# Gated attention and MLP mixer on one core: the last unit's end by halves of queries, two token tiles evicted by ScalarE and POOL, and one weight block copied instead of loaded

## The chip, the cores and the metric

The kernel runs on one core of one Trainium2 chip. Its engines are TensorE (PE, matmuls into the eight banks of PSUM), VectorE (DVE), ScalarE (ACT), GpSimd (POOL) and SyncE (SP), each with its own queue of instructions that it takes in order; SP and ACT also issue DMA transfers from their queues. An instruction can stand in its queue waiting for semaphores, and then everything behind it in that queue stands too. The metric is the device time of one execution in microseconds, shown as the median of several runs.

## What is computed

The input is x, 2048 tokens of 448 features. Sixteen attention heads of 28 features share one key and one value head (multi-query attention); beside it stands a mixer with token shifts and an MLP; a sigmoid gate of each token blends both. All of it is float32.

```python
g = _sigmoid((x * gate_w).sum(-1, keepdims=True))
a = _A_ref(x, A_wq, A_wk, A_wv, A_wo)     # attention, then @ wo
b = _B_ref(x, B_w1, B_w2, B_w3, B_w4)     # shifts and MLP
return g * a + (1 - g) * b
# in _A_ref
scores = jnp.einsum("bhqd,bkd->bhqk", q, k) * (Dh ** -0.5)
p = _softmax(scores, axis=-1)
o = jnp.einsum("bhqk,bkd->bhqd", p, v)
# in _B_ref
h2 = _gelu(_layernorm(x1, axis=-1) @ w3) @ w4
return x1 + h2
```

## The kernel before

The first part of the program (to about 165 us) makes queries, keys, values and the token mixing. The second part is the MLP, in four blocks of 512 tokens (`b`) and 14 blocks of 128 hidden features (`f`). Float32 products are done as three products of a rounded high part and a low part (`w4h` and `w4l`, `gh` and `gl`), so each weight block is loaded raw (`raw3`, `raw4` in a tile `w34raw`) and split: ACT writes the high part, DVE the rest (`split_w4`). For the last two hidden blocks of the last token block a plain float32 copy of their w4 rows, `w4f`, is used later (`w4_half`); before the change it comes by a DMA of its own at `b == 2`, `f == 2`.

The third part is the attention, in 16 units `u` (four blocks of 512 queries times four groups of four heads). A unit goes over 16 key tiles `kt` of 128 keys. For each key tile PE makes the scores of the four heads in four PSUM banks (`scores`). ACT takes the exponential of three of them straight from PSUM (`p`); DVE copies the fourth to SBUF (`pd`) and ACT takes its exponential there, two key tiles at once (`late_exps`). PE then multiplies with the values, four heads side by side in 32 columns each, by halves of 256 queries (`value`, `values`); the value tile has a column of ones, so that the sums of the softmax come out as a row. DVE adds each pair of key tiles to an accumulator `o` (`add_value`). Some units later `o` is divided by its sums (`norm`) and multiplied with a quarter of wo (`wo_job` for a token tile of 128, `wo_half` for half its 448 columns); the product, times the gate, is added to the output tile `ot_n`, and after the fourth group the tile is stored.

That eviction has two forms. `by_one` is one DVE instruction: bank times gate plus `before`. `by_two` is an ACT instruction that writes bank times gate to a tile `y`, and a POOL addition of `y` to `ot`. Before the change `by_two` serves one tile, token tile 0 of the last unit, and there is one tile `y`.

The end of the program (from `toks = ...`) treats the last two key tiles (14 and 15) of the last unit, u = 15. Its accumulator is normalised in a shorter way than the others: PE transposes `o` by token tiles so that the sums lie along partitions (`tail_sums`), DVE takes reciprocals and spreads them to 32 columns (`rx`), PE transposes them back (`tail_spread`), and DVE multiplies `o` with them (`on`). `tail_sums(0)` and `tail_spread(0)` serve the first half of the queries (token tiles 0 and 1), those with 1 the second (2 and 3). Between them stand the last two halves of unit 14's product (`wo_half(u - 1, 3)` and `wo_half(u - 1, 7)`), and then the four `wo_job` of unit 15, whose tiles `ot_12` to `ot_15` are stored by four DMAs: `ot_12` and `ot_14` from ACT's queue, `ot_13` and `ot_15` from SP's. At the very end DVE writes a flag `redo` (all sums were in range), each engine loads it and branches, and SP waits for the DMA semaphores.

The order of instructions on each engine is that of the program text: the schedule is manual. PSUM banks are handed out by a list `banks`: `take()` takes the first, and a bank is appended when its last reader has been issued.

Of the kernel before, what the change touches and what calls it, by code (L numbers as in the profile page):

```python
# [9 lines left out]
F32 = mybir.dt.float32  # L10
F32R = mybir.dt.float32r
AF = mybir.ActivationFunctionType
ALU = mybir.AluOpType
# [3 lines left out]
P = 128  # L17
S = 2048
D = 448
# [5 lines left out]
NT = S // P  # L25
NF = F // P
NE = D // 32
NG = H // 4
SCALE = DH ** -0.5
# [8 lines left out]
def f32(ap):  # L38
    return ap.bitcast(F32)
# [3 lines left out]
def gated_mix_kernel(  # L43
# [206 lines left out]
    with tc.tile_pool(name="s1b", bufs=1) as s1b, \  # L250
# [347 lines left out]
        def split_w4(i):  # L598
            nc.scalar.copy(w4h[i], raw4[i])
            nc.vector.tensor_tensor(w4l[i], raw4[i], f32(w4h[i]), ALU.subtract)  # L600

# [44 lines left out]
    with tc.tile_pool(name="s2", bufs=1, reuse_waits="tile") as s2, \  # L646
# [47 lines left out]
        for b in range(NB):  # L694
            acc = [ps2.tile([P, 512], F32, tag="acc", bufs=4, name=f"acc_{b}_{t}") for t in range(4)]
            gs = {}
            for f in range(NF):
# [22 lines left out]
                if b == NB - 1 and f == 4:  # L720
                    weigh_x1(0, 4 * b)
                if b == 2 and f == 2:
                    nc.sync.dma_start(w4f, w4[(NF - 2) * P:NF * P, :].rearrange("(c p) n -> p c n", p=P))
                if b == 1 and f in (0, 2, 4, 6):
# [44 lines left out]
    with tc.tile_pool(name="s3", bufs=1, reuse_waits="tile") as s3, \  # L769
# [53 lines left out]

        ot_of = {}

        def by_two(n, ps, before, cols):
            nc.scalar.activation(y, ps[:, cols], AF.Copy, scale=gg[:, n:n + 1])
            nc.gpsimd.tensor_tensor(ot_of[n], y, before, ALU.add)

# [25 lines left out]

        def wo_half(u, i, then=None):
            t, h = divmod(i, 2)
            wo_job(u, t, slice(224 * h, 224 * h + 224), then=then)

# [77 lines left out]
        pd_free = [s3.tile([P, 2, 512], F32, name=f"pd_{i}") for i in range(PD)]  # L937
        y = s3.tile([P, D], F32, name="y")
        ones1 = s3.tile([P, 1], F32, name="ones1")
# [5 lines left out]
        def turn_of(free):  # L945
            t = free.pop(0)
            free.append(t)
            return t

        def last_exps(kt, bs, parts):  # L950
            ps = p_of[NU - 1, kt] = {j: turn_of(p_free) for j in READ}
            for q in parts:
                for j in READ:
                    nc.scalar.activation(ps[j][:, q], bs[j][:, q], AF.Exp, scale=SCALE)

# [17 lines left out]

        def value(u, kt, q, pv):
            for j in range(4):
                nc.tensor.matmul(pv[32 * j:32 * j + 32, q], vext[:, kt, :], p_of[u, kt][j][:, q],  # L976
                                 start=(kt % 2 == 0), stop=(kt % 2 == 1), tile_position=(0, 32 * j))

# [4 lines left out]
        def values(u, v):  # L983
            if v == 0:
                o_of[u] = s3.tile([P, 512], F32, tag="o", bufs=2, name=f"o_{u}")
            for q in HALVES:
                pv = take()
                for kt in (2 * v, 2 * v + 1):
                    value(u, kt, q, pv)
# [55 lines left out]
        def tail_sums(i):  # L1045
            ps = take()
            for k in range(2):
                nc.tensor.transpose(ps[:, P * k:P * k + P], o[:, toks[2 * i + k]], ident)
            sums = ps[:, 0:2 * P].rearrange("p (k j d) -> p k j d", k=2, j=4)[:, :, :, 0]
            nc.vector.reciprocal(rr[:, i], sums)  # L1050
            nc.vector.tensor_copy(rx[:, i], rr[:, i].unsqueeze(3).broadcast_to([P, 2, 4, 32]))
            return sums, ps
# [14 lines left out]
        toks = [slice(t * P, (t + 1) * P) for t in range(4)]  # L1067
        bs = [scores(u, kt) for kt in (NT - 2, NT - 1)]
        last_exps(NT - 2, bs[0], [slice(0, 512)])
        banks.extend(bs[0][j] for j in READ)  # L1070
        last_exps(NT - 1, bs[1], HALVES)
        values(u, v - 1)
        pvs = [take(), take()]
        for i, q in enumerate(HALVES):
            value(u, NT - 2, q, pvs[i])
        value(u, NT - 1, HALVES[0], pvs[0])
        add_value(u, HALVES[0], pvs[0])
        wo_half(u - 1, 3)
# [83 lines left out]
```

## Time and profile before

| what | value |
|---|---|
| median of 3 runs | 913.67 us (913.38 to 913.93) |
| the profiled execution's own time | 914.09 us |
| its span, first to last instruction | 912.3 us |
| busy: DVE, ACT, POOL | 542.5, 633.4, 106.7 us |
| DMA traffic | 52.27 MB, mean 57 GB/s |
| mean granted TensorE clock | 0.999 |

The span leaves out 1.79 us of the execution's own time (914.09 - 912.3), which lie before the first and after the last instruction. The timeline of an engine gives start, duration, line, operation, the tiles written and read, and in brackets the idle time before it and what ended it; rows with "x8" merge that many instructions that follow one another. The table of windows gives each engine's busy time in a stretch of the span, the granted clock, the share in which the DMA engines were busy, and the bytes they moved per second.

### The profile page before, as it was taken

What the parts mean: (1) busy time and instruction counts of PE and PEld (TensorE: products, weight loads), DVE (VectorE), ACT (ScalarE), POOL (GpSimd) and SP (SyncE); (2) the same over time, 40 slices, a digit from 0 to 9 for tenths busy, and PEclk for the clock granted to TensorE, in tenths of its full rate; (3) what the DMA queues carried; (4) which work ended last, traced back from release to release, by engine and by line L of the source; (5) the groups of instructions that cost most, each with busy time, mean ns of one, the idle gap of its engine ahead of it and who ended that gap; (6) DMA issues with size and microseconds to landing.
All of it is one profiled execution on the core that took longest, in us unless ns stands there. A gap on an engine that the chain in (4) does not pass through costs nothing.

```text
span 912.3 us, 24128 instructions
## 1 busy us (share of the span) xinstructions
PE 905.2 (99%) x10093; PEld 642.2 (70%) x10093; DVE 542.5 (59%) x1086; ACT 633.4 (69%) x1134; POOL 106.7 (12%) x138
## 2 busy tenths in 40 slices
PE   9999999999999999999999999999999999999997
PEld 7788888888888888875565565556556555655663
DVE  4665264631435736456666766666667766666774
ACT  5442255322232232159999999999999999999994
POOL 3143200212000430002200000000000000000000
PEclk9999999999999999999999999999999999999999
DMA  9832543220222042120000001000011000110001
GB/s 299 271 101 44 158 149 122 40 67 21 41 80 60 21 103 62 37 65 14 26 26 3 26 14 57 24 26 26 6 43 46 26 3 26 29 53 3 15 14 43
DMA packets 42080, 52.27 MB, mean 57 GB/s; under 512 B 9328, under 2 KB 27824, under 8 KB 41968
## 3 DMA queue, kind: packets, MB, share of 16 engines
q1 hardware_dynamic: 38800, 45.00, 17.5%
q10 hardware_dynamic: 3168, 5.70, 1.8%
q8 instruction: 80, 1.31, 0.6%
q14 instruction: 32, 0.26, 0.1%
HBM read 37.50 MB, written 11.93 MB: 54 GB/s over the span
## 4 chain that ended last, share of the span: by engine, by line
PE 99%; ACT 0%; DVE 0%; issue 0%; DVEq 0%; ACTq 0%
PE bank L976 24%; PE bank L933 22%; PE bank L840 8%; PE acc L691 5%; PE acc L690 5%; PE acc L692 5%; PE g L132 4%; PE g L131 4%; PE g L133 4%; PE hs L460 1%; PE hs L461 1%; PE g L134 1%; PE g L135 1%; PE h L131 1%; PE h L132 1%; PE h L133 1%
## 5 line engine op out<-in xcount | busy, mean ns | idle before, releaser
L966 ACT ACTIVATE p<-bank 128x512 f32<-128x512 f32 x762 | 386.9, 617 | 1.5 <-PE bank L933 1.5
L976 PE MATMUL bank<-p,vext 128*32 128x256 f32 x3080 | 243.7, 379 | 0.0
L976 PE MATMUL bank<-pd,vext 128*32 128x256 f32 x1016 | 240.1, 379 | 0.0
L963 DVE COPY pd<-bank 128x512 f32<-128x512 f32 x254 | 175.3, 691 | 51.0 <-PE bank L933 50.0
L976 PEld LDWEIGHTS bank<-p,vext 128*32 128x32 f32 x3080 | 126.0, 110 | 81.9 <-ACT p L966 0.5
L679 ACT ACTIVATE gh<-g 128x512 fp32r<-128x512 f32 x54 | 32.3, 597 | 181.6 <-PE g L135 181.6
L980 DVE TENSOR_TENSOR o<-o,bank 128x256 f32<-128x256 f32 x224 | 94.4, 421 | 93.3 <-ACT p L966 54.0
L971 ACT ACTIVATE pd<-pd 128x1024 f32<-128x1024 f32 x127 | 140.9, 1109 | 0.0
L933 PE MATMUL bank<-qh,kH 30*128 30x512 f32 x1024 | 116.8, 443 | 0.0
L976 PEld LDWEIGHTS bank<-pd,vext 128*32 128x32 f32 x1016 | 111.6, 110 | 0.0
L682 DVE TENSOR_TENSOR gl<-gf,gh 128x512 fp32r<-128x512 f32 x54 | 37.2, 689 | 118.7 <-ACT gf L680 118.6
L933 PE MATMUL bank<-ql,kH 28*128 28x512 f32 x1024 | 103.6, 390 | 0.0
L933 PE MATMUL bank<-qh,kL 28*128 28x512 f32 x1024 | 103.5, 391 | 0.0
L933 PEld LDWEIGHTS bank<-qh,kH 30*128 30x128 f32 x1024 | 60.2, 182 | 57.4 <-ACT p L966 46.0
L691 PE MATMUL acc<-w4l,gh 128*128 128x448 f32 x216 | 79.0, 366 | 0.0
L690 PE MATMUL acc<-w4h,gh 128*128 128x448 f32 x216 | 78.9, 365 | 0.0
L692 PE MATMUL acc<-w4h,gl 128*128 128x448 f32 x216 | 78.7, 365 | 0.0
L840 PE MATMUL bank<-wof,on 128*32 128x224 f32 (+1 forms) x992 | 72.9, 370 | 0.0
L132 PE MATMUL g<-al,w3h 128*128 128x512 f32 x168 | 65.8, 392 | 0.0
L131 PE MATMUL g<-ah,w3h 128*128 128x512 f32 x168 | 65.6, 391 | 0.0
L133 PE MATMUL g<-ah,w3l 128*128 128x512 f32 x168 | 65.5, 390 | 0.0
L933 PEld LDWEIGHTS bank<-ql,kH 28*128 28x128 f32 x1024 | 50.9, 186 | 9.3
(202 smaller groups left out, 1165.6 us busy)
## 6 DMA issues: line engine op xcount, KB each, us to landing
qd<-qf ACTq DMA_DIRECT2D x16, 256.0 KB
qm<-qd SPq DMA_DIRECT2D x16, 256.0 KB
qr<-qd SPq DMA_DIRECT2D x16, 256.0 KB
rb<-rd SPq DMA_DIRECT2D x15, 256.0 KB
x<-in_x_dram SPq DMA_DIRECT2D x4, 896.0 KB
xd<-xt SPq DMA_DIRECT2D x16, 224.0 KB
w34raw<-in_w_dram SPq DMA_DIRECT2D x7, 512.0 KB
w34raw<-in_w_dram SPq DMA_DIRECT2D x7, 448.0 KB
```

What stands on the lines that cost most here:

```text
L131: nc.tensor.matmul(ps, wh[:, c, :], ah[:, c, :], start=(c == 0), stop=False)
L132: nc.tensor.matmul(ps, wh[:, c, :], al[:, c, :], start=False, stop=False)
L133: nc.tensor.matmul(ps, wl[:, c, :], ah[:, c, :], start=False, stop=False)
L690: nc.tensor.matmul(ps, gh[:, tok], w4h[i][:, k, :], start=(f == 0), stop=False)
L691: nc.tensor.matmul(ps, gh[:, tok], w4l[i][:, k, :], start=False, stop=False)
L692: nc.tensor.matmul(ps, gl[:, tok], w4h[i][:, k, :], start=False, stop=(f == stop))
L840: nc.tensor.matmul(ps[32 * j:32 * j + 32, cols], on_of[u][:, tok], wof[:, g, cols], start=True, stop=True, tile_position=(0, 32 * j))
L933: nc.tensor.matmul(bs[j], w, a, start=(i == 0), stop=(i == 2), tile_position=(32 * j, 0))
L963: nc.vector.tensor_copy(ps[j], bs[j])
L966: behind[kt % 2] = nc.scalar.activation(ps[j], bs[j], AF.Exp, scale=SCALE)
L971: ins = nc.scalar.activation(pd, pd, AF.Exp, scale=SCALE)
L976: nc.tensor.matmul(pv[32 * j:32 * j + 32, q], vext[:, kt, :], p_of[u, kt][j][:, q], start=(kt % 2 == 0), stop=(kt % 2 == 1), tile_position ...
```

## The change

Three things change.

First, the weight copy. `split_w4` of the last block (at `b == 0`, `f == 9`) has ACT write `w4f` from the raw tile that is there anyway; the DMA of `w4f` at `b == 2` goes.

Second, the end by halves. Key tiles 12 and 13 of the last unit are no longer added to `o` by themselves: for each half of the queries, key tiles 12 to 15 are accumulated in one bank (`pvs`, the banks of two score tiles of key tile 14) and added once. The exponentials of tiles 14 and 15 are ordered by halves of queries, except one bank that is needed whole; DVE copies one score bank of tile 14 to SBUF (`pd`). The first half's accumulation is finished before the second half's tile 14.

Third, the evictions. `wo_half(u - 1, 3)` and `wo_job(u, 1)`, both of `ot_13`, go by `by_two`, with two tiles `y` in turn; `wo_half(u - 1, 7)` moves behind the block that holds key tile 15's second half; the banks of `tail_spread` are others; `wo_job(u, 3)` stands before the product that makes the flag.

```diff
         def split_w4(i):
             nc.scalar.copy(w4h[i], raw4[i])
+            if 2 * i + 2 == NF:
+                nc.scalar.copy(w4f, raw4[i])
             nc.vector.tensor_tensor(w4l[i], raw4[i], f32(w4h[i]), ALU.subtract)
...
-                if b == 2 and f == 2:
-                    nc.sync.dma_start(w4f, w4[(NF - 2) * P:NF * P, :].rearrange("(c p) n -> p c n", p=P))
...
+        spread_of = []
         def by_two(n, ps, before, cols):
-            nc.scalar.activation(y, ps[:, cols], AF.Copy, scale=gg[:, n:n + 1])
-            nc.gpsimd.tensor_tensor(ot_of[n], y, before, ALU.add)
+            y = turn_of(y_free)
+            ins = nc.scalar.activation(y[:, cols], ps[:, cols], AF.Copy, scale=gg[:, n:n + 1])
+            if spread_of:
+                tc.add_manual_dep(ins.ins, spread_of.pop().ins.name, SYNC, reason="POOL's addition behind DVE's copy")
+            nc.gpsimd.tensor_tensor(ot_of[n][:, cols], y[:, cols], before, ALU.add)
...
-        y = s3.tile([P, D], F32, name="y")
+        y_free = [s3.tile([P, D], F32, name=f"y_{i}") for i in range(2)]
...
             nc.vector.reciprocal(rr[:, i], sums)
-            nc.vector.tensor_copy(rx[:, i], rr[:, i].unsqueeze(3).broadcast_to([P, 2, 4, 32]))
+            copy = nc.vector.tensor_copy(rx[:, i], rr[:, i].unsqueeze(3).broadcast_to([P, 2, 4, 32]))
+            if i == 0:
+                spread_of.append(copy)
...
-        bs = [scores(u, kt) for kt in (NT - 2, NT - 1)]
-        last_exps(NT - 2, bs[0], [slice(0, 512)])
-        banks.extend(bs[0][j] for j in READ)
-        last_exps(NT - 1, bs[1], HALVES)
-        values(u, v - 1)
-        pvs = [take(), take()]
+        b14, b15 = [scores(u, kt) for kt in (NT - 2, NT - 1)]
+        p14 = p_of[u, NT - 2] = {j: turn_of(p_free) for j in range(DRAIN)}
+        p14[DRAIN] = turn_of(pd_free)[:, 0, :]
+        p15 = p_of[u, NT - 1] = {j: turn_of(p_free) for j in range(4)}
+        nc.vector.tensor_copy(p14[DRAIN], b14[DRAIN])
+        nc.scalar.activation(p14[0], b14[0], AF.Exp, scale=SCALE)
+        for q in HALVES:
+            for p, ps in [(p14[1], b14[1]), (p14[2], b14[2]), (p14[DRAIN], p14[DRAIN])] + [(p15[j], b15[j]) for j in READ]:
+                nc.scalar.activation(p[:, q], ps[:, q], AF.Exp, scale=SCALE)
+        assert not banks
+        pvs = [b14[0], b14[DRAIN]]
         for i, q in enumerate(HALVES):
-            value(u, NT - 2, q, pvs[i])
-        value(u, NT - 1, HALVES[0], pvs[0])
+            for kt in (NT - 4, NT - 3):
+                value(u, kt, q, pvs[i], kt == NT - 4, False)
+        value(u, NT - 2, HALVES[0], pvs[0], False, False)
+        value(u, NT - 1, HALVES[0], pvs[0], False, True)
+        banks.extend((b14[1], b14[2]))
         add_value(u, HALVES[0], pvs[0])
-        wo_half(u - 1, 3)
+        value(u, NT - 2, HALVES[1], pvs[1], False, False)
         later = []
-        wo_half(u - 1, 7, later)
+        wo_half(u - 1, 3, by_two, later)
         held = [tail_sums(0)]
         with tc.block():
             tc.mark_branch_hint_location("redo", "LikelyTaken", [mybir.EngineType.PE])
-            value(u, NT - 1, HALVES[1], pvs[1])
+            value(u, NT - 1, HALVES[1], pvs[1], False, True)
+        banks.extend(b15)
+        later.pop(0)()
+        wo_half(u - 1, 7, by_one, later)
         add_value(u, HALVES[1], pvs[1])
-        banks.extend(bs[1][j] for j in READ)
         tail_spread(0)
         held.append(tail_sums(1))
         later.pop()()
...
-        wo_job(u, 1)
+        wo_job(u, 1, evict=by_two)
         wo_job(u, 2, queue=nc.scalar)
+        wo_job(u, 3)
         tw = bank("worst_t")[0:1, 0:1]
         nc.tensor.matmul(tw, worst, ones1, start=True, stop=True)
         nc.vector.tensor_scalar(redo, tw, P - 0.5, None, op0=ALU.is_lt)
-        wo_job(u, 3)
```

Where PE's queue ends differently (an UNCONDITIONAL_BRANCH marks the begin or end of a program block): the stretch around key tile 15's second half (`p_10` to `p_13` before, `p_9` to `p_12` after; `on_14` is unit 14's normalised output, `o_15` the accumulator). Before:

```order
L840 MATMUL bank_1_3493<-wof_3490,on_14_10755 32x224 [waits DVE_49]
L840 MATMUL bank_1_3493<-wof_3490,on_14_10755 32x224 x3
L840 MATMUL bank_0_3492<-wof_3490,on_14_10755 32x224 [waits DVE_49]
L840 MATMUL bank_0_3492<-wof_3490,on_14_10755 32x224 x3
L1048 MATMUL bank_5_3498<-ident_67,o_15_10617 128x128 [waits DVE_49]
L1048 MATMUL bank_5_3498<-ident_67,o_15_10617 128x128
L1082 UNCONDITIONAL_BRANCH
L1158 BRANCH_PREFETCH_HINT
L976 MATMUL bank_7_3495<-p_10_3514,vext_73 32x256 [waits Activation_49]
L976 MATMUL bank_7_3495<-p_12_3516,vext_73 32x256 [waits Activation_49]
L976 MATMUL bank_7_3495<-p_13_3517,vext_73 32x256 [waits Activation_49]
L976 MATMUL bank_7_3495<-p_11_3515,vext_73 32x256
```

After the change:

```order
L974 MATMUL bank_0_3492<-pd_1_3523,vext_73 32x256 [waits Activation_49]
L844 MATMUL bank_5_3498<-wof_3490,on_14_10756 32x224 x4
L1046 MATMUL bank_7_3495<-ident_67,o_15_10618 128x128 [waits DVE_49]
L1046 MATMUL bank_7_3495<-ident_67,o_15_10618 128x128
L1090 UNCONDITIONAL_BRANCH
L1168 BRANCH_PREFETCH_HINT
L974 MATMUL bank_0_3492<-p_9_3513,vext_73 32x256 [waits Activation_49]
L974 MATMUL bank_0_3492<-p_10_3514,vext_73 32x256 [waits Activation_49]
L974 MATMUL bank_0_3492<-p_11_3515,vext_73 32x256 [waits Activation_49]
L974 MATMUL bank_0_3492<-p_12_3516,vext_73 32x256
L1090 UNCONDITIONAL_BRANCH
L844 MATMUL bank_1_3493<-wof_3490,on_14_10756 32x224 x4
```

One of the two wo halves, four instructions, now stands behind key tile 15's second half, in front of the spreading of the reciprocals, and key tile 14's second half (its last row is the first shown) has moved in front of the other.

ACT's queue from the last exponentials on; `DMA out_0_dram<-ot_12` is the store of the first output tile, with the semaphores that it waits for. Before:

```order
L954 ACTIVATE p_12_3516<-bank_2_3494 128x256
L954 ACTIVATE p_13_3517<-bank_6_3499 128x256
L1082 UNCONDITIONAL_BRANCH x2
L827 ACTIVATE y_3525<-bank_4_3497,gg_75 128x448 [waits PE_49]
L848 DMA out_0_dram<-ot_12_9866 128x448 [waits DMAHW5_49,Pool_49]
L848 DMA out_0_dram<-ot_14_10096 128x448 [waits DMAHW7_49,DVE_49]
```

After the change:

```order
L1076 ACTIVATE p_10_3514<-bank_2_3494 128x256
L1076 ACTIVATE p_11_3515<-bank_6_3499 128x256
L1090 UNCONDITIONAL_BRANCH x2
L829 ACTIVATE y_0_3525<-bank_5_3498,gg_75 128x224 [waits DVE_49,PE_49]
L829 ACTIVATE y_1_3526<-bank_6_3499,gg_75 128x448 [waits PE_49]
L852 DMA out_0_dram<-ot_12_9867 128x448 [waits DMAHW4_49,Pool_49]
L829 ACTIVATE y_0_3525<-bank_5_3498,gg_75 128x448 [waits PE_49,Activation_49]
L852 DMA out_0_dram<-ot_14_10097 128x448 [waits DMAHW5_49,DVE_49]
```

Two ACT instructions for `ot_13` are new, and the second of them stands behind the store of `ot_12`, which waits for POOL.

SP's queue at the same place. Before:

```order
L815 DMA rd_14_10639<-rr_14_10637 128x16 [waits DMAHW3_49,DVE_49]
L817 DMA rb_14_10641<-rd_14_10639 128x1x512 [waits DMAHW5_49,DMAHW3_49]
L1082 UNCONDITIONAL_BRANCH x2
L848 DMA out_0_dram<-ot_13_9983 128x448 [waits DMAHW6_49,DVE_49]
L848 DMA out_0_dram<-ot_15_10219 128x448 [waits DVE_49]
L1101 TENSOR_LOAD redo_10944 [waits DVE_49]
```

After the change:

```order
L815 DMA rd_14_10640<-rr_14_10638 128x16 [waits DMAHW2_49,DVE_49]
L817 DMA rb_14_10642<-rd_14_10640 128x1x512 [waits DMAHW4_49,DMAHW2_49]
L1090 UNCONDITIONAL_BRANCH x2
L852 DMA out_0_dram<-ot_13_9984 128x448 [waits DMAHW6_49,Pool_49]
L852 DMA out_0_dram<-ot_15_10220 128x448 [waits DVE_49]
L1111 TENSOR_LOAD redo_10945 [waits DVE_49]
```

The store of `ot_13` now waits for POOL instead of DVE, and that of `ot_15` stands behind it as before. The four stores take the DMA semaphores in turn; the one named in a row is the one whose earlier use the store waits for, so the stores of `ot_12` and `ot_14` have moved from DMAHW5 and DMAHW7 to DMAHW4 and DMAHW5, and that of `ot_15`, the last, from DMAHW0 to DMAHW7. SP's closing wait takes the eight in the order 0 to 7.

More of the change, by code (lines that the diff above doesn't have):

```diff
@@ L854, in wo_job, with wo_half @@
                 then.append(finish)
-        def wo_half(u, i, then=None):
+        def wo_half(u, i, evict=by_one, then=None):
             t, h = divmod(i, 2)
-            wo_job(u, t, slice(224 * h, 224 * h + 224), then=then)
+            wo_job(u, t, slice(224 * h, 224 * h + 224), evict, then=then)
         def w4_job(t):
@@ L948, in turn_of @@
             return t
[L950 to L954, printed above, removed]
         def exps(u, kt, bs):
@@ L972, in late_exps, with value @@
             tc.add_manual_dep(ins.ins, behind[0].ins.name, SYNC, reason="one wait of ACT for its own writes per stretch")
-        def value(u, kt, q, pv):
+        def value(u, kt, q, pv, start, stop):
             for j in range(4):
                 nc.tensor.matmul(pv[32 * j:32 * j + 32, q], vext[:, kt, :], p_of[u, kt][j][:, q],
-                                 start=(kt % 2 == 0), stop=(kt % 2 == 1), tile_position=(0, 32 * j))
+                                 start=start, stop=stop, tile_position=(0, 32 * j))
         def add_value(u, q, pv):
@@ L988, in values @@
                 for kt in (2 * v, 2 * v + 1):
-                    value(u, kt, q, pv)
+                    value(u, kt, q, pv, kt % 2 == 0, kt % 2 == 1)
                 if v == 0:
```

## The prediction

> **What bounds the kernel now.** I read the page, then windows by stage, then the timelines of the end.
>
> ```profile
> span 912.3 us, 24128 instructions
> PE 905.2 (99%) x10093; PEld 642.2 (70%) x10093; DVE 542.5 (59%) x1086; ACT 633.4 (69%) x1134; POOL 106.7 (12%) x138
> ```
>
> ```profile
> 400.00:896.50 496.50, 496.15 (x8130) 297.33 (x8133) 341.94 (x685) 494.70 (x890) 34.54 (x36) 1.00 0.09 26
> 896.50:901.10 4.60, 4.60 (x85) 2.54 (x80) 1.43 (x4) 4.28 (x12) 0.00 (x0) 1.00 0.00 0
> 901.10:907.60 6.50, 5.54 (x54) 1.75 (x50) 5.36 (x18) 0.63 (x1) 1.14 (x1) 1.00 0.13 47
> 907.60:910.40 2.80, 0.00 (x0) 0.00 (x0) 0.00 (x0) 0.00 (x0) 0.00 (x0) 0.96 0.67 239
> 910.40:912.30 1.90, 0.00 (x0) 0.00 (x0) 0.00 (x0) 0.00 (x0) 0.00 (x0) 0.50 0.00 0
> ```
>
> Each window has the busy times of PE, PEld, DVE, ACT, POOL, then granted clock, DMA share, GB/s. Until 901.1 PE has no hole. After it PE and DVE alternate (5.54 and 5.36 of 6.50 us); from 907.6 only the stores run, then nothing but queues. So the change can move the last 11 us alone, and of them the 4.7 after 907.6 only by when the stores are issued.
>
> PE's part of the end:
>
> ```profile
> 898.90 1.48 PE L976 MATMUL bank<-p,vext 128*32 128x256 f32 x24
> 900.20 0.94 PE L840 MATMUL bank<-wof,on 128*32 128x224 f32 x16
> 901.07 0.44 PE L1048 MATMUL bank<-ident,o 128*128 128x128 f32 x2
> 901.44 0.64 PE L976 MATMUL bank<-p,vext 128*32 128x256 f32 x8
> 902.14 0.44 PE L1057 MATMUL bank<-ident,rx 128*128 128x128 f32 x2
> 902.69 0.44 PE L1048 MATMUL bank<-ident,o 128*128 128x128 f32 x2
> 903.06 0.96 PE L840 MATMUL bank<-wof,on 128*32 128x448 f32 x8
> 903.95 0.44 PE L1057 MATMUL bank<-ident,rx 128*128 128x128 f32 x2
> 904.31 1.71 PE L840 MATMUL bank<-wof,on 128*32 128x448 f32 x16
> ```
>
> Eight matmuls, one key tile's half, take 0.43 us of PE's queue ((900.20 - 898.90) / 3), a wo half 0.38, a whole wo job 0.75. DVE's and the others' part:
>
> ```profile
> 898.35 0.42 DVE L980 TENSOR_TENSOR o<-o,bank 128x256 f32<-128x256 f32 x1 [2.21 <-PE bank L976]
> 900.51 0.42 DVE L980 TENSOR_TENSOR o<-o,bank 128x256 f32<-128x256 f32 x1 [0.87 <-ACT p L954]
> 901.79 0.29 DVE L1051 COPY rx<-rr 128x256 f32<-128x256 f32 x1
> 902.22 0.42 DVE L980 TENSOR_TENSOR o<-o,bank 128x256 f32<-128x256 f32 x1
> 905.42 1.44 DVE L831 SCALAR_TENSOR_TENSOR ot<-bank,gg,ot 128x448 f32<-128x448 f32 x2
> 906.90 0.68 DVE L831 SCALAR_TENSOR_TENSOR ot<-bank,gg,ot 128x448 f32<-128x448 f32 x1
> ```
>
> ```profile
> 896.50 4.28 ACT L954 ACTIVATE p<-bank 128x512 f32<-128x512 f32 x12 [0.28 <-PE bank L933]
> 904.09 0.63 ACT L827 ACTIVATE y<-bank,gg 128x448 f32<-128x448 f32 x1 [3.30 <-PE bank L840]
> 904.79 1.14 POOL L828 TENSOR_TENSOR ot<-y,ot 128x448 f32<-128x448 f32 x1 [100.30 <-ACT y L827]
> 905.97 0.34 ACTq L848 DMA_DIRECT2D out_dram<-ot  x1
> 906.89 0.34 ACTq L848 DMA_DIRECT2D out_dram<-ot  x1
> 907.61 0.34 SPq L848 DMA_DIRECT2D out_dram<-ot  x1
> ```
>
> The stores of ot_12 (905.97) and ot_14 (906.89) are ACT's, that of ot_15 (907.61) is SP's. To be seen: three DVE evictions from 905.42 to 907.58, and the last store right behind.
>
> **The change part by part.** *The weight copy costs nothing.* ACT writes 128x896 once more, behind the cast of the same size:
>
> ```profile
> 169.22 0.94 ACT L599 CAST w4h<-w34raw 128x896 fp32r<-128x896 f32 x1
> 171.60 0.60 ACT L679 ACTIVATE gh<-g 128x512 fp32r<-128x512 f32 x1 [1.44 <-PE g L135]
> 256.97 0.42 SPq L723 DMA_DIRECT2D w4f<-in_w_dram  x1
> ```
>
> ACT sits idle 1.44 us there for PE, and a copy of the cast's size needs 0.94; without that cover it would delay a gelu by 0.94 us, and PE, full, would lose part of it. The removed load took 0.42 us of SP's queue, 650 us before the end. PE is full in both places: 0.
>
> *The halves bring about 0.36 us.* PE does the same matmuls up to 898.90 (key tiles 12 and 13). Then key tile 15's first half comes at 899.33 instead of 899.77, its addition 0.43 us earlier than 900.51. Is ACT ready? From the rows of its last exponentials
>
> ```profile
> L954 ACT ACTIVATE p<-bank 128x256 f32<-128x256 f32 x8 | 2.4, 465 | 0.0
> L954 ACT ACTIVATE p<-bank 128x512 f32<-128x512 f32 x4 | 2.1, 603 | 0.3 <-PE bank L933 0.3
> L963 DVE COPY pd<-bank 128x512 f32<-128x512 f32 x254 | 175.3, 691 | 51.0 <-PE bank L933 50.0
> ```
>
> a 512 follows another after 0.50 us ((2.1 - 0.60) / 3), a 256 after 0.28 ((2.4 - 0.47) / 7). One 512 and seven 256 put the first half's last exponential at 896.50 + 0.50 + 6 x 0.28 = 898.7, done at 899.1: in time. Key tile 14's second half, now next on PE at 899.77, needs the tenth 256, done at 900.0: PE waits up to 0.2. The wo half for ot_13 ends near 900.7 instead of both halves at 900.96, and the transposes start there instead of 901.07. Key tile 15's second half follows near 901.1; the last exponential (896.50 + 0.50 + 13 x 0.28 + 0.47 = 901.1, in place of 900.78) is just in time. The other wo half (0.38), moved behind it, now stands before the spreading: that starts at 901.9 for 902.14, the accumulator's second addition at 901.8 for 902.22, the second transposes at 902.3 for 902.69. From there everything has the old lengths: wo_job(0) at 902.7, y at 903.73, POOL until 905.58, the store of ot_12 at 905.61 in place of 905.97. Bounds: 0.43 if ACT never holds PE, 0.1 if it does at both places.
>
> *DVE is relieved.* It loses a half eviction, a whole one (0.68) and two additions, and gains one copy of a score bank (0.69 by the group L963), in the 2.21 us idle before 898.35. ot_14 then waits for PE only: wo_job(2), moved by 0.36, is done at 905.66 and evicted by 906.43; ot_15 by 907.18 in place of 907.58.
>
> *The two-engine evictions lose it again.* POOL's queue gets half of ot_13 (between 0.57, half of 1.14, and 1.14; I take 0.6) from 902.2 to 902.8, free long before 904.44. But in ACT's queue the scaling of ot_13 stands behind the store of ot_12, and that waits for POOL until 905.58. So: store 905.61, the next ACT instruction 0.38 later at 905.99, 0.63 long; POOL 0.08 later, 906.70 to 907.84; SP's store of ot_13 at 907.87. Behind it in SP's queue stands the store of ot_15, ready since 907.18: it goes at 908.26 (0.34 and 0.05 between). ot_14's store, next in ACT's queue, goes at 906.6. **The last store leaves 0.65 us later than before (907.61), though DVE is ready 0.4 earlier.** Had ACT not been held, y for ot_13 would be done by 905.6 and POOL by 906.75.
>
> *What a later store costs.* The stores and the closing:
>
> ```profile
> 906.75:907.00 0.25, 0.06 (x4) 0.00 (x0) 0.25 (x3) 0.00 (x0) 0.00 (x0) 1.00 0.68 258
> 907.00:908.00 1.00, 0.00 (x0) 0.00 (x0) 0.59 (x1) 0.00 (x0) 0.00 (x0) 1.00 1.02 375
> 909.30:909.60 0.30, 0.00 (x0) 0.00 (x0) 0.00 (x0) 0.00 (x0) 0.00 (x0) 1.00 0.49 139
> L1103 SPq COMPARE_BRANCH  x1: 45/45/45, 909.1 to 909.1; - x1
> L1103 SPq EVENT_SEMAPHORE  x8: 17/17/17, 910.4 to 910.9; - x8
> ```
>
> Data start about 0.83 us behind the first issue (905.97 to 906.8), and run at 375 GB/s: a tile of 128 x 448 x 4 bytes takes 0.61, the four 2.45, to 909.25. That stream was the limit before: alone, the last would have ended at 907.61 + 0.83 + 0.61 = 909.05. After, ot_13 has the engines from 908.70 to 909.31 and ot_15 ends at 909.93: 0.67 later. Then SP waits for the eight DMA semaphores one by one, from 910.4 to 910.9, 1.1 us behind the last of the data. Before, the last store holds the first of the eight, and seven more steps (0.5 us) follow; after, it holds the eighth, and the seven can be passed while it lands. SP's branch, tied to the store's place in its queue, comes at 909.8 (909.1 + 0.65), so the eighth is reached at 910.3 or later, however long SP takes after the branch (before, at most 1.2). Landing at 910.3 to 911.0 (0.4 to 1.1 behind the data, the row's 1.1 being the upper end) then passes the eighth wait at 910.3 to 911.0, against 910.9: between -0.6 and +0.1; if the whole closing simply moves with the store, +0.65. I take -0.1: 1.1 was one execution's, and the profiled one was 0.42 us above the median (914.09 against 913.67).
>
> The Trainium skill, "DMA: Bandwidth & Descriptors", section on the anatomy of one DMA, gives a fixed 2.0 us and bytes / 436 GB/s. By it, as an estimate, the last store would land at 908.26 + 2.53 = 910.8; the trace's bounds hold that, and the sum would be 0.0 instead of -0.1.
>
> **Sum:** 914.09 - 0.1 in the profiled execution's terms, so 913.6 against the median of 913.67: no change that can be told (0.2%, 1.8 us, is about what a measurement of this kernel can tell from none). Its own range is -0.8 to +0.6.
>
> **Rivals.** *ACT is not held* (it goes past the store, or POOL is done sooner): the last store leaves at 907.2, the stream runs from 906.44 to 908.9, and with the closing's order 0.9 is gained: 912.8. For it: the bank for ot_13's y is ready by 905.0. Against: ACT's two stores and its y stand in one queue, and no row shows it pass a waiting one. 8%.
>
> *POOL's additions are slow* (the other side). The same shape has taken more than 1.14:
>
> ```profile
> L392 POOL TENSOR_TENSOR wsum<-w1raw 128x448 f32<-128x448 f32 x1 | 1.5, 1516 | 12.1 <-DMA w1raw<-in_w_dram 12.1
> ```
>
> Two of them are now in series before the last store, so 2 x 0.37 us come on top: 914.4. It decides from 1.2 us an addition. For it: DVE is at work during both. Against: it was at work beside the 1.14 too. 13%. The Trainium skill, "SBUF — State Buffer", section on the two separate sides, has VectorE and GpSimd share a pair of ports that one of them locks for a whole instruction; by it the last addition could wait out the eviction of ot_15, up to 907.2, which would give 914.1.
>
> *The halves do not come earlier* (the change doesn't do what it says): ACT holds PE at both places, the chain gains 0.1 for 0.36, and the rest stands: 913.9. 11%.
>
> *Something outside the end moves* (placement of tiles, fetching of instructions) by more than 1.8 us, either way: no row speaks for it, but none of the trace of before can exclude it either, since 0.2% of PE's 905 us would do. 10%, half of it each way.
>
> **How the numbers follow.** The forecast has 58%. Its range and the two rivals at 912.8 and 914.4 give 912.8 to 914.5 for eight in ten. Faster by over 0.2% needs 911.8: the unseen, 5%. Slower by over 0.2% needs 915.5: the unseen, or two mishaps at once, 6%. The rest, 89%, lies within.
>
> **What would show it.** The step on ACT is right if its second y starts right behind a store, about 0.4 us after POOL's end, and SP's last two stores stand within 0.4 us of each other near 908; it is wrong if y precedes POOL's end. The halves are right if wo_job(0) starts near 902.7 and DVE's last eviction ends near 907.2. The closing is right if SP's eight waits are spread out, the last at 910.3 to 911.0. A hole in PE before 899 or near 171 would make the forecast wrong.

## The result, and the profile after

| | us |
|---|---|
| before, median of 15 runs beside the change | 913.9 (913.38 to 914.45) |
| after the change, median of 15 runs | 915.67 (915.08 to 916.85) |
| ratio, 95% interval | 1.002 (1.0012 to 1.0027) |
| the profiled execution of after: own time, span | 915.08, 913.3 |

The change loses 1.8 us, with an interval of 1.1 to 2.5; no change had been forecast, and the time lies above the range. The first lines of the page after:

```profile
span 913.3 us, 24128 instructions
PE 904.5 (99%) x10093; PEld 643.2 (70%) x10093; DVE 541.5 (59%) x1083; ACT 635.5 (70%) x1140; POOL 108.9 (12%) x140
```

The span grew by 1.0 only, less than the time, because this execution was ahead of the one of before when the end began. The last score matmuls, in the timelines of PE of before and of after:

```profile
896.78 0.42 PE L933 MATMUL bank<-ql,kH 28*128 28x512 f32 x4
```

```profile
896.08 0.41 PE L937 MATMUL bank<-ql,kH 28*128 28x512 f32 x4
```

So 0.70 us must be added to the times of after before they stand beside those of before. From these matmuls to the span's end it is 15.5 us before and 17.2 after: the end alone has lost 1.7, as much as the medians say. The windows of that end (busy PE, PEld, DVE, ACT, POOL, granted clock, DMA share, GB/s):

```profile
900.80:907.70 6.90, 5.12 (x56) 1.86 (x48) 4.36 (x16) 1.72 (x3) 2.93 (x3) 1.00 0.19 69
907.70:908.50 0.80, 0.00 (x0) 0.00 (x0) 0.00 (x0) 0.00 (x0) 0.00 (x0) 1.00 0.00 0
908.50:909.70 1.20, 0.00 (x0) 0.00 (x0) 0.00 (x0) 0.00 (x0) 0.00 (x0) 0.83 1.02 363
909.70:910.40 0.70, 0.00 (x0) 0.00 (x0) 0.00 (x0) 0.00 (x0) 0.00 (x0) 0.50 0.22 31
910.40:911.95 1.55, 0.00 (x0) 0.00 (x0) 0.00 (x0) 0.00 (x0) 0.00 (x0) 0.50 0.11 27
```

Two things are new. Before, the stores' data ran in one stream; now there are 0.8 us without any, since two stores come late. And behind the last of the stream (909.70) come 2.2 us in which a little is still moved, at about 30 GB/s.

Why the stores are late, in the timelines of ACT, of POOL, and of SP and DVE:

```profile
903.43 0.63 ACT L829 ACTIVATE y<-bank,gg 128x448 f32<-128x448 f32 x1 [1.60 <-PE bank L844]
905.32 0.34 ACTq L852 DMA_DIRECT2D out_dram<-ot  x1
905.76 0.63 ACT L829 ACTIVATE y<-bank,gg 128x448 f32<-128x448 f32 x1 [1.69 <-PE bank L844]
906.16 0.34 ACTq L852 DMA_DIRECT2D out_dram<-ot  x1
```

```profile
904.14 1.14 POOL L832 TENSOR_TENSOR ot<-y,ot 128x448 f32<-128x448 f32 x1 [1.58 <-ACT y L829]
906.53 1.13 POOL L832 TENSOR_TENSOR ot<-y,ot 128x448 f32<-128x448 f32 x1 [1.24 <-issue]
```

```profile
907.68 0.81 SPq L852 DMA_DIRECT2D out_dram<-ot  x2
905.44 1.44 DVE L835 SCALAR_TENSOR_TENSOR ot<-bank,gg,ot 128x448 f32<-128x448 f32 x2 [0.82 <-PE bank L844]
```

Read from the top: POOL adds ot_12 until 905.28; ACT's store of it follows at 905.32; the scaling of ot_13, whose product PE had long finished, starts only behind that store, at 905.76; POOL adds it until 907.66; SP stores it at 907.68, and ot_15, which DVE had ready at 906.88, goes behind it (the trace has it at 908.07). "PE bank" in the bracket of 905.76 is the last semaphore event that the instruction named, not what held it.

PE, from the last key tiles on:

```profile
898.65 0.82 PE L974 MATMUL bank<-p,vext 128*32 128x256 f32 x11
899.52 0.76 PE L844 MATMUL bank<-wof,on 128*32 128x224 f32 x8
900.20 0.44 PE L1046 MATMUL bank<-ident,o 128*128 128x128 f32 x2
900.57 0.64 PE L974 MATMUL bank<-p,vext 128*32 128x256 f32 x8
901.03 0.56 PE L844 MATMUL bank<-wof,on 128*32 128x224 f32 x8
901.52 0.44 PE L1057 MATMUL bank<-ident,rx 128*128 128x128 f32 x2
902.41 0.96 PE L844 MATMUL bank<-wof,on 128*32 128x448 f32 x8 [0.21 <-DVE on L1060]
```

With 0.70 added, the transposes (L1046) start at 900.90 for 901.07, but the first spreading (L1057) at 902.22 for 902.14, and wo_job(0), the last row, at 903.11 for 903.06. The halves are worth nothing. Matmuls of 32 columns start in sets of four, 0.2 us apart; in the trace the fourth of a set of key tile 14, which waits for the exponential of `pd` (ACT until 899.23), starts at 899.27, 0.18 behind its three companions, and the sets behind it stay torn up to the transposes: the eight of the wo half (second row) start between 899.52 and 899.92, where in before eight start within 0.21.

Last the closing, SP's eight waits of before, from 910.4 to 910.9, and of after:

```profile
L1113 SPq EVENT_SEMAPHORE  x8: 17/17/17, 910.1 to 911.9; - x8
```

Seven are passed from 910.1 on; the eighth, that of ot_15's store, at 911.9, and the span ends 1.4 later. A store is finished by sixteen completions. Of ot_15's, thirteen stand between 910.06 and 910.24 in the trace, and three at 911.53, 911.85 and 911.90: 3.83 us after the issue. Before, the slowest of the last store came at 910.37, 2.75 after its issue.

The loss in the end, from the two traces: the last store leaves 1.16 later (11.97 for 10.81 after the last score matmul), its last completion takes 1.08 longer (3.83 for 2.75), and the closing behind that completion is 0.54 shorter: 1.70.

### The profile page after: what moved, and what is told of

Its sections match the earlier page's. It is cut to its first block, busy times and chain, and to the rows that moved or that the text cites. A ratio compares the mean times of both kernels' runs of the same rounds, so it can differ in the third digit from the quotient of the medians.

```text
span 913.3 us, 24128 instructions
## 1 busy us (share of the span) xinstructions
PE 904.5 (99%) x10093; PEld 643.2 (70%) x10093; DVE 541.5 (59%) x1083; ACT 635.5 (70%) x1140; POOL 108.9 (12%) x140
```

## The experiments

Each kernel was timed in five rounds beside the kernel before; "before" in the table is the median of that chip. By time alone w4_only, store_sp, one_by_dve, after_noflag, spread_first, turn_kept and two_act cannot be told from before, since their intervals reach 1; those of store_sp and one_by_dve end below the one of the change (1.0012 to 1.0027). What lies within is read from the traces.

| kernel | median us | before | ratio, 95% interval |
|---|---|---|---|
| w4_only | 913.53 | 914.14 | 0.9993 (0.9984 to 1.0002) |
| end_only | 916.58 | 914.14 | 1.0028 (1.0018 to 1.0039) |
| store_sp | 913.48 | 914.14 | 0.9995 (0.9986 to 1.0004) |
| one_by_dve | 913.17 | 914.14 | 0.9993 (0.9984 to 1.0002) |
| before_noflag | 912.75 | 914.2 | 0.9984 (0.9975 to 0.9993) |
| after_noflag | 913.91 | 914.2 | 0.9998 (0.9989 to 1.0007) |
| late_store | 915.01 | 914.2 | 1.0012 (1.0003 to 1.0021) |
| spread_first | 913.8 | 914.2 | 0.9998 (0.9989 to 1.0007) |
| copy_and_turn | 916.35 | 914.12 | 1.0025 (1.0014 to 1.0035) |
| dve_act | 912.94 | 914.12 | 0.999 (0.9981 to 0.9999) |
| two_act | 912.99 | 914.12 | 0.9991 (0.9982 to 1.0) |
| turn_kept | 913.87 | 913.88 | 0.9999 (0.999 to 1.0008) |

**The two parts alone.** w4_only is the kernel before with the weight copy:

```diff
             nc.scalar.copy(w4h[i], raw4[i])
+            if 2 * i + 2 == NF:
+                nc.scalar.copy(w4f, raw4[i])
...
-                if b == 2 and f == 2:
-                    nc.sync.dma_start(w4f, w4[(NF - 2) * P:NF * P, :].rearrange("(c p) n -> p c n", p=P))
```

> The kernel before with the weight block w4f copied by ScalarE instead of loaded, nothing else. Theory A (the loss sits behind the last store: ScalarE's second y stands behind a waiting store, so the last store leaves about 1.1 us later, and lands another 1.1 us later still) expects no loss here, and a gain of up to 0.5 us, 913.4 to 913.9, because the removed load turns the DMA semaphores by one and the last store then holds the eighth instead of the first of SP's eight closing waits. Rival B (the weight copy costs the time) expects about +1.8 us, 915.7.

end_only is the change with these lines as they were before.

> The changed kernel with the load of w4f put back. Theory A expects the whole loss, and 0.5 us more of it since the last store holds the first of the closing waits again: +1.8 to +2.3 us, 915.7 to 916.2. Rival B expects the time of before, 913.9.

The parts add up: -0.6 and +2.4 make the +1.8 of the change. So the whole loss, and more, is in the end, and the weight copy costs nothing and seems to gain a little. end_only lies 0.4 above what was expected for it: in its trace the last store lands 4.24 us after its issue, for 3.83 in the change.

**The held scaling.** store_sp takes the store of ot_12 out of ACT's queue:

```diff
-        wo_job(u, 0, evict=by_two, queue=nc.scalar)
+        wo_job(u, 0, evict=by_two)
```

> The changed kernel with the store of ot_12 issued from SP's queue, so that ScalarE's y of ot_13 stands behind no store. Theory A expects y at once after its product, POOL's two additions back to back, the last store about 1.1 us earlier than in the change (as in before), and 913.4 to 914.0. Rival C (PE's new order at the end costs the time: the first half's reciprocals are spread later than before) expects no more than 0.2 us back: 915.4.

one_by_dve leaves that store and takes ot_13 back from ACT and POOL:

```diff
-        wo_job(u, 1, evict=by_two)
+        wo_job(u, 1)
```

> The changed kernel with wo_job(u, 1), the whole second half of ot_13's sum, evicted by VectorE in one instruction as before; the half before it stays with ScalarE and POOL. Theory A expects three evictions in a row on VectorE as before and the last store where it was before: 913.4 to 914.0. Rival C expects 915.4.

ACT's second y in store_sp, and SP's two stores in one_by_dve:

```profile
905.17 0.64 ACT L829 ACTIVATE y<-bank,gg 128x448 f32<-128x448 f32 x1 [0.69 <-PE bank L844]
```

```profile
906.00 1.77 SPq L852 DMA_DIRECT2D out_dram<-ot  x2
L1113 SPq EVENT_SEMAPHORE  x8: 17/17/17, 909.5 to 910.0; - x8
```

In store_sp y starts 0.69 behind the first y's end, not 1.69, before POOL has finished ot_12 (905.70), and all the loss is gone: 913.48. So it is the store in ACT's queue that holds it. one_by_dve removes the same wait by removing its waiter: the last store leaves 10.78 us after the last score matmul (10.81 before), all its completions are in by 909.61, the eight waits are over at 13.37 (14.12 before), and the time is 913.17, 0.2 below the range expected. Each counted from the before of its own chip, these are 2.4 and 2.7 us better than the change: more than the 1.16 by which the store was late.

**What a late store meets.** Amid the data of the last store, instructions are fetched. The DMA queues in a window that ends with the stores' stream, of before (906 to 909.3) and of after (906.3 to 909.7); columns are packets, MB, and the share of sixteen engines:

```profile
q10 hardware_dynamic: 288, 0.46, 37.7%
q1 hardware_dynamic: 273, 0.45, 37.6%
```

```profile
q10 hardware_dynamic: 265, 0.42, 33.1%
q1 hardware_dynamic: 241, 0.40, 33.0%
q8 instruction: 1, 0.02, 1.8%
q14 instruction: 2, 0.02, 1.1%
```

Three packets of instructions, two of 8 KB and one of 16 KB, start in after's stream, 1.7 us behind the branches on the flag (907.7). In before the same three start from 909.32 on, where the stream has only its last 0.3 us to go, and delay little: fifteen completions of the last store are in by 909.93, and one comes at 910.37. In after it is not the store alone that moved: with 0.70 added, its first packet of instructions starts 0.78 later than in before, but the last store leaves 1.16 later.

The window behind the stream, 909.86 to 911.45 in after, shows whose data still move there:

```profile
DMA packets 25, 0.05 MB, mean 29 GB/s; under 512 B 3, under 2 KB 24, under 8 KB 24
q1 hardware_dynamic: 24, 0.04, 13.1%
```

q1 carries the stores from SP's queue, so it is the last store itself: 0.04 MB is about three sixteenths of its 0.23 MB, and the three small packets close the three shares that are late. The single packets of the trace agree. Each of the four stores is 128 packets of 1,792 bytes; in after seven of these 512 take more than 0.2 us, up to 0.54, all of them from 909.76 on, and in before none takes more than 0.14. The store of ot_13, just ahead, has three late completions as well (910.01 to 910.40, the others by 909.63).

The packets of instructions come with the code behind the flag, the fallback that recomputes units. Two kernels leave out that flag's test and the fallback, one of before and one of after:

```diff
-            tc.mark_branch_hint_location("redo", "LikelyTaken", [mybir.EngineType.PE])
...
-        again = nc.values_load(redo, min_val=0, max_val=1)
-        with tc.If(again > 0, label="redo"):
...
```

> The kernel before without the load of the flag, the branch and the fallback behind it (it leaves out the redo of units whose sums are out of range). Theory D (what delays a late last store is the fetching of instructions that starts about 1.2 to 1.7 us after the engines' branch and takes three of the DMA engines) expects no such fetches among the stores, or at another place, and the landings of the last store within 0.3 us of one another: 913.0 to 913.8 against 914.1 of before. Rival E (stores that are issued close together on one queue land late by themselves) expects no difference here either.

> The changed kernel without flag, branch and fallback. Theory D expects the late issue to stay (about 1.1 us) but no late landing: 0.5 to 0.7 us above the kernel before without the flag, after the closing order gives 0.5 back. Rival E expects the last store to land 3.8 us after its issue as in the change: 1.5 us or more above the kernel before without the flag.

Without the fallback the change costs 1.16 us (913.91 against 912.75), the 1.12 by which its last store is later there (11.95 for 10.83), and nothing else. That is between what D and E expected. D's 0.5 to 0.7 counted on the closing's order, which gives nothing here: the span ends 0.84 us behind the last completion for 0.89 in before_noflag, where with the flag it is 1.40 for 1.94. E's late landing is not there. The window up to 911.9 of after_noflag has no row of instructions,

```profile
q1 hardware_dynamic: 288, 0.46, 22.2%
q10 hardware_dynamic: 288, 0.46, 22.1%
```

and all sixteen completions of its ot_15 stand within 0.18 us (910.92 to 911.10), 2.0 to 2.2 after the issue; the three late ones are gone, and in neither of the two kernels does a packet of 1,792 bytes take more than 0.10 us. These two also lack the loads of the flag and the branches. The test with the branch left in: late_store makes the last store late in the kernel before (with the weight copy, so that its closing order is after's), by two additions on DVE whose result nobody reads.

```diff
+        for i in range(2):
+            nc.vector.tensor_add(p_free[i], o, on_of[u])
         wo_job(u, 3)
```

> The kernel before with w4f copied by ScalarE and two additions of 128x512 that nobody reads on VectorE in front of ot_15's eviction, so that the last store leaves about 1.2 to 1.3 us later; the other three stores and the branches of the other engines stay. Theory D expects more than the delay itself: some landings 1 us or more behind the others, and 915.5 to 916.3, 2.0 us or more above the same kernel without the additions (913.5). Rival E (it has no other store near it on its queue) expects the delay alone, 914.8.

DVE's last rows, and the DMA queues in the window from 906 to 909.9:

```profile
906.42 1.27 DVE L1101 TENSOR_TENSOR p<-o,on 128x512 f32<-128x512 f32 x2
907.62 0.67 DVE L831 SCALAR_TENSOR_TENSOR ot<-bank,gg,ot 128x448 f32<-128x448 f32 x1
```

```profile
q1 hardware_dynamic: 269, 0.43, 32.0%
q10 hardware_dynamic: 288, 0.46, 31.9%
q8 instruction: 1, 0.02, 2.0%
q14 instruction: 2, 0.02, 1.5%
```

The last store leaves at 11.95 after the last score matmul for 10.83 in w4_only, 1.12 later, and meets the three fetches; thirteen of its completions stand at 910.11 to 910.26, three at 910.62, 911.27 and 911.43. Its end, from the last score matmul, is 1.64 us longer than w4_only's: the 1.12, and 0.51 for the landing, 3.11 us after the issue instead of 2.60. The time, 915.01, misses both expectations and lies nearer to E's 914.8 than to D's 915.5 to 916.3; the trace decides for D's mechanism at half the price: a store that is late for another reason has three of sixteen completions late too, if fetches run beside its data, and six of its packets take 0.2 to 0.44 us. Which of the sixteen DMA engines carried a fetch the trace does not name, so that the three late completions are on the three engines of the three fetches is inferred from the count.

**The halves.** spread_first is store_sp with the other wo half put behind wo_job(0), so that nothing stands in front of the first spreading:

```diff
-        wo_half(u - 1, 7, by_one, later)
...
-        later.pop()()
         wo_job(u, 0, evict=by_two)
+        wo_half(u - 1, 7, by_one)
```

> The changed kernel with the store of ot_12 on SP's queue and the half of unit 14's product that the change had put in front of the first spreading moved behind wo_job(u, 0). Theory F (that half, 0.38 us on PE, is what took the halves' gain) expects the first spreading 0.2 us earlier and wo_job(u, 0) about 0.25 us earlier, measured from the end of the last scores, and the last store where it was, since PE works through from there: within 0.3 us of 913.5. If the halves themselves bring nothing, wo_job(u, 0) stays where it was.

PE's rows in store_sp, then in spread_first:

```profile
900.62 0.44 PE L1046 MATMUL bank<-ident,o 128*128 128x128 f32 x2
901.94 0.44 PE L1057 MATMUL bank<-ident,rx 128*128 128x128 f32 x2
902.83 0.96 PE L844 MATMUL bank<-wof,on 128*32 128x448 f32 x8 [0.21 <-DVE on L1060]
```

```profile
900.99 0.44 PE L1046 MATMUL bank<-ident,o 128*128 128x128 f32 x2
902.13 0.44 PE L1057 MATMUL bank<-ident,rx 128*128 128x128 f32 x2
902.95 1.34 PE L844 MATMUL bank<-wof,on 128*32 128x448 f32 x16
```

From the transposes to the spreading it is 1.32 with the half between and 1.14 without, to wo_job(0) 2.21 and 1.96: the moved half costs 0.25 us. It only moved the loss, though: the later jobs come 0.12 later, and the time is no better.

**The closing's order.** w4_only gained 0.6 by leaving out a load that stands 650 us before the end. In its trace the last store holds the eighth of SP's waits, as in the change. Two kernels copy the weights and keep the load's turn among the semaphores: copy_and_turn loads 16 bytes a partition into a new small tile,

```diff
-                    nc.sync.dma_start(w4f, w4[(NF - 2) * P:NF * P, :].rearrange("(c p) n -> p c n", p=P))
+                    nc.sync.dma_start(spare, w4[(NF - 2) * P:(NF - 1) * P, 0:4])
...
+        spare = late.tile([P, 4], F32, name="spare")
```

> The kernel before with w4f copied by ScalarE, and in place of its load a load of 128x4 elements into a tile that nobody reads, so that the DMA semaphores turn as before and the last store holds the first of SP's eight closing waits. Theory G (the 0.6 us that the weight copy alone gave come from the order of the closing waits) expects the time of before, within 0.2 us of 914.1, and seven waits in a row, 0.5 us, behind the last landing. Rival H (they come from the removed load itself) expects 913.5.

and turn_kept loads the same values once more into w4f itself, with no new tile:

```diff
+                    nc.sync.dma_start(w4f[:, 0, 0:4], w4[(NF - 2) * P:(NF - 1) * P, 0:4])
```

> The kernel before, with ScalarE's copy of w4's last plain tiles in place of their load, and where the load stood a load of 16 bytes a partition into the same tile: the same values again, so SP keeps its turn among the DMA semaphores and no tile is added. Theory G (the load's 0.6 us came from the order of the closing waits, which the load's turn sets): the tail, from the start of the last score matmul to the span's end, is 15.5 us as before, with seven waits of SP in a row behind the last landing, and the time is 914.1 +-0.3. Rival (it came from the load's own traffic or its place in SP's queue, and the missing turn did nothing): tail 14.8, 913.5. On the 2.2 us that the tiny load into a new 16-byte tile cost in the stage of the experts: if the new tile did it, by moving the tiles after it, they are gone here; if the tiny load or its wait did it, the time is 916.3 again.

SP's waits of w4_only and of turn_kept:

```profile
L1103 SPq EVENT_SEMAPHORE  x8: 17/17/17, 909.2 to 909.8; - x8
```

```profile
L1105 SPq EVENT_SEMAPHORE  x8: 17/17/17, 910.1 to 910.6; - x8
```

From the last score matmul these are 12.84 to 13.44 in w4_only, 13.33 to 13.87 in turn_kept, 13.55 to 14.09 in copy_and_turn and 13.58 to 14.12 before: with the load's turn kept, seven waits follow the last completion again, 0.54 us in all, and turn_kept takes the time of before (913.87 and 913.88). So it is the order, and nothing is left for the load's traffic to explain. turn_kept's last completion came 0.25 us sooner than before's, which its time does not show; the seven waits behind the landing stand in all three traces with the load's turn, and not in w4_only's.

copy_and_turn's 2.2 us were a surprise, and none of it is in its end. Most of it, 1.8 of the row below, arises while the MLP's matmuls run (the expectation calls the MLP the experts), which take longer there than in before and in turn_kept; the same line of the three, in that order (min, median, max in ns):

```profile
L132 PE MATMUL g<-al,w3h x168: 387/390/398, 124.6 to 396.6; 128*128 128x512 f32 x168
```

```profile
L132 PE MATMUL g<-al,w3h x168: 388/393/398, 125.0 to 398.8; 128*128 128x512 f32 x168
```

```profile
L132 PE MATMUL g<-al,w3h x168: 389/389/398, 124.4 to 396.7; 128*128 128x512 f32 x168
```

turn_kept has the same tiny load at the same place and loses nothing, so it was the 16-byte tile and not the load. That it acts by moving the tiles behind it to other addresses is likely, but was not tried.

**Better versions.** In both of these, ot_15's store goes to ACT's queue: dve_act is one_by_dve with that, two_act is store_sp with it.

```diff
-        wo_job(u, 3)
+        wo_job(u, 3, queue=nc.scalar)
```

> The changed kernel with wo_job(u, 1) evicted by VectorE and the last store, ot_15's, issued from ScalarE's queue, so that SP's load of the flag does not stand behind it. Theory A (what counts is when the last store lands and when SP reaches the eighth wait) expects the last store where it is without this (10.8 us behind the last scores), SP's waits reached up to 0.4 us earlier, and 912.7 to 913.2, below before and the change. If the landing alone counts, 913.2 as without it.

> The changed kernel with the store of ot_12 on SP's queue and that of ot_15 on ScalarE's: ScalarE's y of ot_13 is held by no store, and ot_15's store does not stand behind ot_13's. Theory A expects the last store 0.1 us earlier than with ot_12's store moved alone, SP's waits 0.4 us earlier, and 913.0 to 913.5. A rival is that ScalarE's queue, which then issues the last two stores and loads its flag behind them, branches later, and its fetch of instructions meets no store: no change by that.

Both medians are some 1.1 us below before, 0.999 (0.9981 to 0.9999) and 0.9991 (0.9982 to 1.0), which is only just told from none for the first and not for the second, and 2.9 below the change. How much of it is the queue is not settled: against one_by_dve it is 0.2 us. In two_act the last store leaves at 10.78 for 10.91 in store_sp.

## Why the prediction was wrong

The times of after have 0.70 added here, so that they stand beside those of before and of the prediction.

| event | before | predicted | after |
|---|---|---|---|
| first transposes | 901.07 | 900.7 | 900.90 |
| first spreading | 902.14 | 901.9 | 902.22 |
| wo_job(0) | 903.06 | 902.7 | 903.11 |
| store of ot_12 | 905.97 | 905.61 | 906.02 |
| POOL done with ot_13 | | 907.84 | 908.36 |
| ot_15 evicted by DVE | 907.58 | 907.18 | 907.58 |
| last store issued | 907.61 | 908.26 | 908.77 |
| its last completion | 910.37 | 910.3 to 911.0 | 912.60 |

- *The weight copy costs nothing*: right for PE and ACT. That the load's turn among the semaphores sets the closing was said, but under the later store; it is the weight copy's own gain, 0.54 us by w4_only and turn_kept.
- *The halves bring about 0.36 us*: wrong. They bring -0.05, outside the bounds of 0.43 and 0.1. The transposes came 0.17 earlier instead of 0.37. The wait for key tile 14's exponential was there, 0.18, and the torn sets carry it on to the transposes. The prediction named up to 0.2 for it and counted about half (899.77 + 0.43 + 0.38 is 900.58, and it took 900.7), and it left out the 0.11 that before has between the end of its wo halves and the transposes (900.96 to 901.07). The moved wo half then took the rest: 1.32 from the transposes to the spreading, where 1.2 was reckoned and 1.07 is before's. spread_first shows 0.25 us for that half, up to wo_job(0).
- *DVE is relieved*: the instructions are fewer, yet ot_15 is ready when it was, since PE's products come when they did.
- *The two-engine evictions lose it again*: right, and the main cause. y starts 0.48 behind POOL's end, predicted 0.41; the two stores of SP are 0.39 apart. The last store left 1.16 late instead of 0.65: 0.41 from the halves' missing gain, 0.10 from gaps between store, y, POOL and store that are a little longer. store_sp and one_by_dve show it by the wait's removal.
- *The later store's cost, -0.1*: the step that failed. The order of the closing gave its 0.5, but the landing was bounded by 1.1 us behind the data, from one execution in which the fetches came at the stream's last 0.3 us. That 1.1 held some of their price already: without the fallback the same store lands 2.14 us after its issue in before_noflag, for 2.75 in before. What a store that moves further into the fetches pays was a term that the sum did not have. The last completion stands 2.2 us behind the stream's end (909.70 to 911.90), not 0.4 to 1.1. after_noflag shows it by their absence and late_store by another late store. Of the 1.8 by which the end missed its forecast (+1.70 for -0.1), 0.51 is the later issue, and 1.29 this step: +0.54 behind the issue, where -0.75 was reckoned. Without the fetches a store that is 1.12 late costs 1.16, in the pair without the flag. The price is not a constant: landings with fetches at the stream's end or in it took from 2.60 (w4_only) to 4.24 us (end_only), and what sets it was not tried.
- The fixed cost of a transfer that the prediction took from the Trainium skill, "DMA: Bandwidth & Descriptors", section on the anatomy of one DMA, put the last store's landing 2.53 us after the issue. That section is on DMAs from GpSimd's queue, and this store is from SP's. Undisturbed, in after_noflag, the trace has 2.0 to 2.2, and with fetches 3.83: neither is the rule's figure, which has no term for what else the DMA engines carry.
- *POOL's additions are slow* (a rival): no. They took 1.14 and 1.13 with DVE at work beside them. The Trainium skill's page "SBUF — State Buffer", section on the two separate sides, has the shared port locked by a VectorE instruction in a two-port mode or with two inputs from SBUF; an eviction reads one of its two tiles from PSUM, so the prediction took the rule more widely than the page has it. No lock shows in the rows: the second addition started at 906.53, before the eviction's end at 906.88.
- *ACT is not held* (a rival): no, as the change stands; store_sp makes it true by other means and comes to 913.48.
- *The halves do not come earlier* (a rival): true as to the size, -0.05 for its 0.1, but not as it was meant. PE was held at one place and not at two, and the moved half took the rest. Its price, 913.9, leaves most of the loss open.
- *Something outside the end moves* (a rival): no. The end's 1.70 is the medians' 1.8.

## What to carry to other kernels

A DMA trigger that waits stands in its engine's queue like any instruction: before work is put behind it, look at what it waits for, and give the store to a queue in which nothing else is due. A last store has a second price beyond its lateness, what else uses the DMA engines at its new time, and instruction fetches behind a branch were among that here; look at the queue rows of the end, not at the stores' alone. Where a program closes by waiting for its semaphores one by one, the store that lands last should hold the last turn. Removing one transfer shifted that turn here, 650 us before the end.

## What the runs showed of the hardware

- Fetches of 8 and 16 KB of instructions, under way beside a store's data, made three of its sixteen completions 1.3 to 1.7 us later than the others (after), 0.4 to 1.2 in late_store. Packets of 1,792 bytes took up to 0.54 us then, and at most 0.10 where nothing was fetched.
- Without the flag's test and the fallback the kernel before is 1.45 us shorter (912.75 against 914.2). In the traces the last store lands 0.6 sooner, and 1.05 less follow its landing (0.89 for 1.94).
- SP passes a closing wait that is already fulfilled in 0.07 to 0.1 us: seven of them are 0.54.
- One more tile of 16 bytes a partition made the kernel 2.2 us slower, with the MLP's matmuls of one line at a median of 393 ns for 390; in its absence the same small load cost nothing.
